# Softmax denominators inverted by pow on GpSimd instead of a reciprocal on VectorE, in a kernel whose engine orders come from a cost model

## Chip, cores, metric

One core of one Trainium2 chip. The metric is the device time of one execution in microseconds. Timed runs of the kernel before and of the other kernel alternate on the same chip. PE is TensorE, DVE is VectorE, ACT is ScalarE, POOL is GpSimd, SP is SyncE, whose sequencer ("the issue queue", SPq in the profile) issues every DMA of this kernel.

## The reference, cut to what matters

Two layers. Each is sliding-window attention (2048 tokens, 32 heads of 16, window 256) and a token-mixing MLP with 1792 hidden units; before each stands a layer norm (a double one for the MLP).

```python
scores = einsum("bhqd,bhkd->bhqk", q, k) * (Dh ** -0.5)
p = softmax(where(mask, scores, -1e9), axis=-1)          # the denominators are of this softmax
o = einsum("bhqk,bhkd->bhqd", p, v)
x = x + o @ wo
...
x = x + B(layernorm(x))                                  # w1, gelu, w2 over the token axis
```

## The kernel before

The program is a graph of some 2,400 operations. Each has a price (`cost`, and for a DMA `issue` and `lat`). A list scheduler simulates the engines with these prices and fixes the order of every engine; two tables of whole numbers (`RANK`, `MOVES`) then shift priorities and places. They look like the outcome of a search on the same prices, and I call them annealed; the search itself is not in the file. The program issues each engine's list in that order, with waits on semaphores. So a price is never executed: it only decides what stands behind what.

```python
def _pick(self, e, cand, ready, free, mode):   # which operation engine e takes next, by simulated time
...
o.end = free[e] = m + o.cost                   # the engine is held for the price
o.done = o.end + (o.lat if o.lat is not None else self.LAT[e])
...
def reorder(self, moves):
    for e, mv in zip(self.ENGS, moves):
        if mv:
            self.order[e] = [self.order[e][i + d] for i, d in enumerate(mv)]
...
for o in self.order[e]:                        # emit: in order, with waits
    for s, v in waits[o.idx]:
        eng.wait_ge(sem(s), v)
    ins = o.fn(eng)
```

The route of the denominators, once for each of 30 groups of heads and queries. P times V leaves numerators and denominators in PSUM; DVE copies both to SBUF (`cs`).

```python
o_rr = op("sync", ... rr[:, tr.slot, 0, :], cs[16:P:32, tc.slot] ..., dma=True, cost=300, lat=1400.0, issue=570.0)
for r in range(4):                             # second half of the heads up to its rows
    op("sync", ... cs[32*r+16:32*r+32, tc.slot, 0, :], cs[32*r:32*r+16, tc.slot, 1, :], dma=True, ..., after=[o_rr])
op("vector", lambda e: e.reciprocal(rr[:, tr.slot, 1, :], rr[:, tr.slot, 0, :]), cost=330)      # 128 x 32
op("sync", ... rscr <- rr[:, tr.slot, 1, :], dma=True)                                          # to DRAM
op("sync", ... md <- rscr broadcast to 16 rows each, dma=True)                                  # and back
op("gpsimd", lambda e: e.tensor_tensor(oT[:, to.slot, :], cs[:, tc.slot, 0, :], md[:, tm.slot, :], op=ALU.mult), cost=1400)
```

The tiles are few: 3 for `cs`, 2 each for `rr` and `md`, 7 for `oT`. GpSimd also makes the masked copies of the keys (`kbd`), `rstd` of every layer norm (with a pow of one or two elements) and some copies of V, all in one order with the output tiles `oT`.

The softmax here doesn't subtract the row's maximum and nothing guards it: scores larger than these inputs give would overflow.

Of the kernel before, what the change touches and what calls it, by code (L numbers as in the profile page):

```python
# [7 lines left out]
dt = mybir.dt  # L8
ALU = mybir.AluOpType
ACTF = mybir.ActivationFunctionType  # L10

P = 128
# [4 lines left out]
W2F, W2OUT = 2, (3, 7)  # L17
# [4 lines left out]
    38, 478, -248, -93, 7, 6, -38, -55, 0, -12, 14, -1, -14, 17, 7, 49, 0, 0, -11, -57, -29, 12, -32, 17, 163, -113,  # L22
    -26, 0, -76, 48, 174, -114, 0, -155, 72, 0, 0, 91, 0, -197, -108, 0, -146, 0, 0, -43, -29, -200, 193, 102, 0,
    116, -16, 0, -1, 11, -60, 21, -73, 18, 2, -2, 7, 89, 40, -31, -47, -15, 10, 0, -22, -49, 42, 322, -14, 6, 33, 2,
    0, 13, 12, 0, -17, -8, -15, 0, 5, -20, 0, 0, 0, -65, 142, 93, 62, -58, 23, 23, -51, -8, -30, 20, 27, 0, -36,
    -55, 10, 8, 0, 76, 151, 136, 83, -40, -3, -176, 115, -122, 460, -486, -53, -30, 29, 53, 0, -45, 0, 0, -39, -32,
    -78, 0, -2, 0, 0, 0, 0, 0, -52, 0, 0, 0, 0, 0, 0, 0, 19, -6, -13, -12, 0, -6, 4, -18, 0, 0, 7, 132, -19, -10,
    -13, 10, 103, -116, 115, -193, 419, 0, 41, 10, 1, 0, -10, 6, -14, -46, 5, -20, 0, 0, 103, -15, 11, 17, 0, 0, -6,
    -79, -112, -156, 0, -7, 0, -468, 0, 0, 0, 2, 0, 17, -7, 9, 6, 12, 0, -28, 0, 45, 117, 31, -17, 0, 0, 0, -19, -6,
    -107, -186, 167, -24, 82, 120, 248, 217, 122, 0, -3, 18, 55, -4, -27, 0, -6, 0, -120, 0, 1, 50, 52, 478, 268, 0,  # L30
    13, 47, 0, -11, 0, 113, 15, 46, 44, -30, -22, -52, 0, 14, -410, 20, 180, -153, -435, -439, 359, -7, 0, -3, 15,
    -10, 13, 10, -4, 12, 0, -86, -10, -52, -43, 17, 227, -51, -403, -135, -167, -266, -230, -240, 44, 0, 0, 4, -190,
    72, 0, 0, 0, 0, 3, 0, -1, 0, 0, 0, 0, 0, 0, 0, 0, 0, 0, 0, 0, 0, 0, 0, 0, 0, 0, 0, 0, 0, 6, 57,
# [3 lines left out]
        7, 1, 3, -2, -1, -1, 4, -1, -8, -1, 1, 3, 3, -4, 2, 3, 3, 0, 2, 2, -8, -8, 0, 0, 0, 0, 2, 0, -2, 0, 0, 2, 0,  # L37
        1, 1, 1, -5, 1, -1, 0, 0, 0, 0, 0, 0, 0, 0, 1, -1, 0, 0, 0, 0, 0, 0, 0, 0, 0, 0, 0, 0, 0, 0, 0, 0, 0, 0, 0,
        0, 0, 0, 0, 0, 0, 1, -1, 0, 0, 0, 0, 0, 0, 0, 0, 0, 0, 0, 0, 0, 0, 0, 0, 0, 0, 0, 0, 0, 0, 0, 0, 0, 0, 0, 0,
        0, 0, 0, 0, 0, 0, 0, 0, 0, 0, 0, 0, 0, 0, 0, 0, 0, 0, 0, 0, 0, 0, 0, 0, 0, 0, 0, 0, 0, 0, 0, 0, 0, 0, 0, 0,  # L40
        0, 0, 0, 0, 0, 0, 0, 0, 0, 0, 0, 0, 0, 0, 0, 0, 0, 0, 0, 0, 0, 0, 0, 0, 0, 0, 0, 0, 0, 0, 0, 0, 0, 0, 0, 0,
        0, 1, -1, 0, 0, 0, 0, 0, 0, 0, 0, 0, 0, 0, 0, 0, 0, 0, 0, 0, 0, 0, 0, 0, 0, 0, 0, 0, 0, 0, 0, 0, 0, 0, 0, 0,
        0, 0, 0, 0, 0, 0, 0, 0, 0, 0, 0, 0, 0, 0, 0, 0, 0, 0, 0, 0, 0, 0, 0, 0, 0, 0, 0, 0, 1, 1, -2, 0, 2, -1, -1,
        0, 1, 3, 3, 4, -4, 1, 4, 4, -5, 0, -8, 1, 1, 1, 2, 0, -8, 0, 2, 7, 7, 1, -4, -2, 4, -6, -3, 2, -4, -4, 0,
        27, -1, 10, 10, 4, 4, -5, -3, 6, -7, -7, 4, -7, 15, -4, 5, -5, -1, -12, 2, 2, 2, -5, -16, -6, -1, -7, 4, 1,
        -4, -4, -1, 0, 0, 0, 0, 0, 0, 0, 3, -1, 2, -1, 1, -4, 1, 1, -2, 0, 0, 1, -1, 0, 0, 0, 0, 0, 0, 0, 0, 0, 1,
        -1, 0, 0, 0, 0, 0, 0, 0, 0, 0, 0, 1, -1, 0, 0, 0, 0, 0, 0, 0, 1, -1, 0, 0, 1, -1, 0, 0, 0, 0, 0, 1, -1, 0,
        0, 1, 1, -2, 0, 0, 0, 0, 0, 0, 0, 0, 0, 0, 0, 0, 0, 0, 0, 0, 0, 0, 0, 1, -1, 0, 0, 0, 0, 0, 0, 0, 0, 0, 0,
        0, 0, 0, 0, 0, 0, 0, 0, 0, 0, 0, 0, 0, 0, 0, 0, 0, 0, 0, 0, 0, 0, 0, 0, 0, 0, 0, 0, 0, 0, 0, 0, 0, 0, 0, 0,
        0, 0, 0, 0, 0, 0, 0, 0, 0, 0, 0, 0, 0, 0, 0, 0, 0, 0, 0, 0, 0, 0, 0, 0, 0, 0, 0, 0, 0, 0, 0, 0, 0, 0, 0, 0,  # L50
        0, 0, 0, 0, 0, 0, 0, 0, 0, 0, 0, 0, 0, 0, 0, 1, -1, 0, 0, 0, 0, 0, 0, 0, 0, 0, 0, 0, 0, 0, 0, 0, 0, 0, 0, 0,
        0, 0, 0, 0, 0, 0, 0, 0, 0, 0, 0, 0, 0, 0, 0, 0, 0, 0, 0, 0, 0, 0, 0, 0, 0, 0, 0, 0, 0, 0, 0, 0, 0, 0, 0, 0,
        0, 1, -1, 0, 1, -1, 0, 1, -1, 0, 0, 0, 0, 0, 0, 0, 0, 0, 0, 0, 0, 0, 0, 0, 0, 0, 3, -1, -1, -1, 4, 0, -2,
        -1, 2, 0, -3, 0, 0, 1, -1, 1, -1, 3, -1, 2, -2, -2, 0, 2, -1, -1, 3, -1, 2, 2, -3, 6, 6, -5, -2, -2, -2, 2,
        2, -4, 1, 4, 0, 0, 2, -1, 1, 1, 1, 1, 1, -15, 1, -1, 3, 3, 3, 20, 3, 3, 0, -7, 1, -8, -8, 16, 7, -3, 1, 1,
        15, 0, 2, 5, -9, 11, -4, -11, -11, -11, -1, -6, 0, 0, 0, 2, -10, 2, -8, 4, 11, -3, 2, -3, 1, -4, -4, 0, 4,
        6, -2, 2, -6, 6, 6, -6, -2, -1, 9, -2, -10, -3, 1, 12, -3, -3, 2, -3, 8, 2, -5, -2, -6, -3, -2, -2, 1, -3,
        5, 0, -2, -1, -1, -1, 0, 0, 0,
    ),
    (  # L60
        7, 4, 4, -2, -4, 6, 6, 6, -4, 5, 6, 4, 7, 7, 3, -7, 2, 4, 4, 4, 4, 4, 5, 10, 24, 1, 3, 13, 3, 5, 0, 1, 4,
        -30, 5, 7, -8, -28, 8, 2, -2, -6, 1, 13, -7, -1, 1, 8, -3, 5, -1, -41, -2, -2, -2, 4, -54, 3, 8, 4, -2, 4,
        -1, -1, 3, 11, -9, 4, 1, -1, 4, -7, 1, 6, 1, 6, 4, 5, -25, -1, 3, 4, 5, 6, 0, 3, 4, 4, 4, -3, 3, 3, 4, -23,
        4, 4, 4, 0, -3, 2, 2, 2, 2, -26, -32, 1, 2, 2, 2, -2, -5, 1, -1, 2, -1, -1, 0, 1, 1, 1, -3, 0, 0, 0, 0, 0,
        1, -1, 0, 0, 0, 0, 0, 0, 0, 1, -1, 0, 0, 0, 1, 1, -2, 0, 1, 1, 1, 2, 0, -5, 1, -1, 0, 2, -1, -1, 0, 2, 0, 1,
        1, 2, -5, 1, 3, 0, 0, -5, 5, 1, -1, 1, 4, 2, -6, -1, 1, 2, 0, 2, 0, 1, 1, -12, 1, 2, -2, 2, 2, 2, -2, 1, 1,
        -7, 0, 0, 0, 0, 0, 0, 0, 1, -1, 0, 0, 0, 1, 1, 1, -3, 0, 0, 0, 2, 0, 1, -3, 0, 2, 0, 1, 3, -4, 3, 3, -2, 3,
        1, 3, 4, 0, 5, 3, 7, 3, 3, 5, 5, 5, -5, -15, -9, -20, -4, 2, 2, 4, 2, 0, -5, 1, 3, -7, -1, -1, 0, 1, 3, -2,
        -1, -1, 1, -1, 0, 0, 0, 0, 0, 0, 0, 1, -1, 0, 0, 0, 1, 1, -2, 0, 0, 0, 0, 1, -1, 0, 0, 0, 0, 0, 0, 0, 0, 0,
        1, -1, 0, 0, 0, 0, 0, 0, 1, 2, 2, 2, 3, 1, -4, -7, 0, 0, 0, 0, 1, -1, 1, -1, 0, 0, 0, 0, 0, 0, 0, 0, 0, 0,  # L70
        0, 0, 0, 0, 0, 0, 0, 0, 1, -1, 2, 0, 2, 3, 3, -5, -1, 5, 3, 1, 3, -8, 2, -5, 1, -6, 0, 0, 0, 0, 0, 2, 0, -2,
        0, 2, 0, 2, -3, -1, 0, 3, -1, -1, 1, 1, 2, 2, -1, -6, 0, 1, -1, 1, 1, -2, 0, 0, 2, 3, 1, 2, 2, 2, 3, 4, 6,
        6, -10, 8, 10, -5, -13, 1, 7, 7, -1, -7, 8, -11, -9, 7, 5, 7, -6, 6, -7, -4, 4, -13, -5, -2, -8, 0, 0, 1,
        -1, 0, 0, 0, 2, 0, -2, 0, 1, 1, 1, 5, 3, 1, 3, 4, 4, 1, 3, -7, 3, 1, -14, 1, 2, 4, -1, 3, -15, -2, 1, -3, 1,
        -1, 3, -1, 2, -2, 3, 3, -1, -1, -6, 1, 2, 2, -1, 2, 2, 4, -7, 0, 0, 1, 1, 1, -8, 0, 0, 0, 0, 2, -1, -1, 0,
        0, 1, 1, -2, 0, 1, -1, 0, 0, 0, 0, 2, 0, 1, 1, 1, 1, 1, 1, 3, 6, 4, 5, 0, 8, -14, 4, 2, 5, -5, 4, 6, -4, 2,
        5, 6, 6, 3, -17, 5, 5, 2, -22, 3, 6, -9, -8, -16, 4, 5, 7, -2, 6, 6, 7, 0, 7, -9, 6, 6, 0, -5, 0, 4, -17, 1,
        2, 2, -17, -16, 0, 0, 0, 0, 0, 1, -1, 0, 2, -1, -1, 0, 0, 0, 0, 0, 0, 0, 0, 0, 0, 1, 1, 1, 1, 1, 1, 1, 1, 2,
        2, 2, -2, 1, 2, 4, 1, 1, -3, 1, 3, 3, 0, 4, 1, -4, 2, -26, 1, -3, 3, 1, -2, 1, 1, 2, 0, -6, 0, 1, 1, 2, 2,
        2, -5, -3, 2, 0, -2, 2, 2, -2, 1, 1, -4, 0, 0, 2, 0, 1, -3, 3, 0, -2, -1, 0, 0, 0, 0, 0, 3, 1, -1, -3, 2, 0,  # L80
        3, 1, -1, 1, 1, 1, 1, 5, -10, -1, 1, 2, -3, -3, 2, 0, 2, 0, -4, 0, 6, 3, 3, 4, 4, 4, 4, -7, -6, -8, 1, -8,
        0, 0, 0, 0, 0, 9, 13, -1, 18, -2, 0, 0, -3, 2, 2, -10, 2, -9, 2, 3, -8, 2, -5, -10, 3, 4, 4, -6, -3, -1, -6,
        1, 1, -2, 2, -1, 2, 0, -3, 0, 0, 0, 0, 0, 0, 3, 0, 0, -3, 0, 0, 1, 1, 3, -3, 2, -1, -3, 1, -1, 0,
    ),
    (
        0, 0, 1, -1, 0, 0, 1, 1, -2, 1, -1, 0, 1, 3, 0, 0, -4, 0, 0, 0, 0, 0, 0, 0, 1, -1, 0, 0, 0, 0, 1, -1, 0, 0,
        0, 0, 0, 0, 0, 0, 0, 0, 1, -1, 0, 0, 0, 0, 0, 0, 0, 0, 0, 0, 0, 0, 0, 0, 0, 0, 0, 0, 1, -1, 0, 0, 0, 0, 0,
        0, 0, 0, 0, 0, 0, 0, 0, 0, 0, 0, 0, 0, 0, 0, 0, 0, 0, 0, 0, 0, 0, 0, 0, 0, 0, 0, 0, 0, 0, 0, 0, 0, 1, -1, 0,
        0, 0, 0, 0, 0, 0, 0, 0, 0, 0, 0, 0, 0, 0, 0, 0, 0, 0, 0, 0, 0, 1, -1, 0, 0, 0, 0, 0, 0, 1, -1, 0, 0, 0, 0,
# [449 lines left out]
def bass_interleave_layers__sliding_block__mixer_token_mlp__prompt_kernel(  # L539
# [21 lines left out]
    with es:  # L561
        sb = lambda name, shape, d=dt.bfloat16: es.enter_context(nc.sbuf_tensor(name, shape, d))
        NKU, NQU, NVU, NPT, NCS, NMD, NOT, NW1, NSTG = 9, 7, 5, 8, 3, 2, 7, 4, 3
        x_sb = sb("x_sb", [P, NT, D])
# [36 lines left out]
        g = Graph(nc, es)  # L601
# [512 lines left out]
```

## Time and profile before

| | before |
|---|---|
| median, range (7 runs of one session) | 484.32 us, 481.53 to 486.41 |
| PE, DVE, ACT, POOL busy in the profiled run (span 481.6 us) | 427.7, 370.0, 322.9, 137.2 us |
| PE idle (span less busy) | 53.9 us |
| granted PE clock | 0.993 |

The lines that carry the reading are in the prediction. One view more, the busy time by stretch, is needed to compare the attention stages (columns: stretch, length, then busy us and instructions for PE, weight load, DVE, ACT, POOL, then granted clock, DMA share, GB/s):

```profile
17.00:180.00 163.00, 134.57 (x2962) 67.41 (x2986) 144.40 (x296) 148.09 (x166) 57.57 (x73) 0.99 0.30 82
232.00:393.00 161.00, 146.52 (x2944) 73.87 (x2972) 136.65 (x281) 137.57 (x150) 52.95 (x69) 0.99 0.34 94
```

GpSimd works about a third of these stages.

### The profile page before, as it was taken

What the parts mean: (1) busy time and instruction counts of PE and PEld (TensorE: products, weight loads), DVE (VectorE), ACT (ScalarE), POOL (GpSimd) and SP (SyncE); (2) the same over time, 40 slices, a digit from 0 to 9 for tenths busy, and PEclk for the clock granted to TensorE, in tenths of its full rate; (3) what the DMA queues carried; (4) which work ended last, traced back from release to release, by engine and by line L of the source; (5) the groups of instructions that cost most, each with busy time, mean ns of one, the idle gap of its engine ahead of it and who ended that gap; (6) DMA issues with size and microseconds to landing.
All of it is one profiled execution on the core that took longest, in us unless ns stands there. A gap on an engine that the chain in (4) does not pass through costs nothing.

```text
span 481.6 us, 15631 instructions
## 1 busy us (share of the span) xinstructions
PE 427.7 (89%) x6763; PEld 209.6 (44%) x6831; DVE 370.0 (77%) x747; ACT 322.9 (67%) x367; POOL 137.2 (28%) x205
## 2 busy tenths in 40 slices
PE   7897887798889698999999899987989979999997
PEld 4453533353334344444554454434444434444443
DVE  6999988988988978665887888888997856951313
ACT  2899999998987860534878978996998862061000
POOL 4223435235422413024102443523374031200000
PEclk9999999999998999999999999998999999999999
DMA  8602221234243344331225422240335235424555
GB/s 243 184 3 71 65 84 39 65 102 134 77 117 109 84 119 121 88 88 44 78 60 129 112 78 71 75 114 9 101 108 167 81 107 163 126 71 120 175 153 176
DMA packets 83993, 49.47 MB, mean 103 GB/s; under 512 B 14676, under 2 KB 78164, under 8 KB 83924
## 3 DMA queue, kind: packets, MB, share of 16 engines
q1 hardware_dynamic: 83924, 48.46, 35.6%
q8 instruction: 54, 0.88, 0.8%
q14 instruction: 15, 0.12, 0.1%
HBM read 41.43 MB, written 2.59 MB: 91 GB/s over the span
## 4 chain that ended last, share of the span: by engine, by line
PE 60%; ACT 14%; DVE 11%; DMA 7%; SPq 3%; issue 3%; POOL 1%; POOLq 0%
PE PS L1037 18%; PE PS L1014 13%; ACT pt L863 13%; PE PS L767 6%; PE PS L896 6%; PE PS L968 5%; PE PS L851 5%; PE PS L797 4%; DVE cs L940 3%; DVE pt L879 2%; DMA cs<-cs 2%; DMA rr<-cs 2%; DVE pt L876 2%; SPq L946 1%; POOL oT L958 1%
## 5 line engine op out<-in xcount | busy, mean ns | idle before, releaser
L863 ACT ACTIVATE pt<-PS 128x1024 bf16<-128x1024 f32 (+1 forms) x304 | 283.9, 1032 | 39.5 <-PE PS L851 37.7
L1014 PE MATMUL PS<-xh_sb,w1b 128*128 128x512 bf16 x428 | 102.9, 380 | 9.3 <-DMA w1b<-in_B_w_dram 3.3
L1037 PE MATMUL PS<-ub,w2b 128*128 128x512 bf16 x429 | 100.6, 379 | 2.8 <-issue 1.3
L851 PE MATMUL PS<-qT,kbd 32*128 32x64 bf16 (+4 forms) x1632 | 61.0, 245 | 17.7 <-ACT pt L863 6.0
L958 POOL TENSOR_TENSOR oT<-cs,md 128x512 bf16<-128x512 f32 x30 | 40.4, 1347 | 100.7 <-DMA md<-rscr 46.3
L1014 PEld LDWEIGHTS PS<-xh_sb,w1b 128*128 128x128 bf16 x448 | 40.1, 98 | 58.8 <-issue 8.9
L1037 PEld LDWEIGHTS PS<-ub,w2b 128*128 128x128 bf16 x448 | 41.6, 98 | 51.1 <-issue 3.3
L879 DVE TENSOR_TENSOR pt<-pt,ldm 128x1024 bf16<-128x1024 bf16 (+1 forms) x80 | 58.4, 732 | 5.8 <-ACT pt L863 5.6
L767 PE MATMUL PS<-xhT,wqkv 128*128 128x512 bf16 x237 | 59.2, 380 | 3.4 <-issue 1.9
L783 POOL TENSOR_SCALAR kbd<-stg,par 128x512 bf16<-128x512 bf16 x56 | 46.0, 829 | 54.4 <-DVE stg L734 49.5
L1026 DVE TENSOR_TENSOR ub<-PS,ub 128x512 f32<-128x512 f32 x70 | 46.1, 684 | 16.5 <-PE PS L1014 16.3
L851 PEld LDWEIGHTS PS<-qT,kbd 32*128 32x128 bf16 x1632 | 23.4, 93 | 72.4 <-ACT pt L863 38.9
L1042 DVE SCALAR_TENSOR_TENSOR x_sb<-PS,bcol,x_sb 128x512 bf16<-128x512 f32 x32 | 23.1, 744 | 39.1 <-PE PS L1037 39.1
L1029 ACT ACTIVATE ub<-ub,bcol 128x512 bf16<-128x512 f32 x28 | 18.5, 713 | 47.2 <-DVE ub L1026 47.1
L940 DVE COPY cs<-PS 128x512 f32<-128x512 f32 x60 | 38.9, 682 | 10.6 <-PE PS L896 10.2
L896 PE MATMUL PS<-pt,vt 64*18 64x64 bf16 (+4 forms) x3040 | 40.9, 248 | 5.7 <-DVE qT L734 1.7
L694 POOL TENSOR_SCALAR rstd<-agg 128x2 f32<-128x2 f32 (+1 forms) x40 | 9.8, 246 | 120.8 <-DVE agg L691 119.8
L689 DVE BATCH_NORM_STATS2 stats<-x_sb 128x6 f32<-128x512 bf16 x64 | 42.7, 681 | 1.1 <-DMA x_sb<-in_A_x_dram 0.6
L876 DVE TENSOR_TENSOR pt<-pt,ldm 128x512 bf16<-128x512 bf16 (+1 forms) x104 | 41.1, 412 | 2.1 <-ACT pt L863 1.7
L896 PEld LDWEIGHTS PS<-pt,vt 64*18 64x18 bf16 x3040 | 32.1, 86 | 16.9 <-DVE pt L876 4.1
L968 PE MATMUL PS<-wo_sb,oT 128*128 128x512 bf16 x118 | 30.9, 388 | 4.8 <-POOL oT L958 2.8
L767 PEld LDWEIGHTS PS<-xhT,wqkv 128*128 128x128 bf16 x256 | 21.8, 98 | 29.5 <-issue 3.3
(54 smaller groups left out, 328.1 us busy)
## 6 DMA issues: line engine op xcount, KB each, us to landing
w1b<-in_B_w_dram SPq DMA_DIRECT2D x56, 256.0 KB, 3.1
w2b<-in_B_w_dram SPq DMA_DIRECT2D x112, 128.0 KB, 2.4
md<-rscr SPq DMA_DIRECT2D x30, 256.0 KB
cs<-cs SPq DMA_DIRECT2D x120, 32.0 KB, 2.8
out_dram<-x_sb SPq DMA_DIRECT2D x16, 128.0 KB, 1.8
x_sb<-in_A_x_dram SPq DMA_DIRECT2D x3, 512.0 KB
wqkv<-in_A_wqkv_dram SPq DMA_DIRECT2D x2, 384.0 KB, 6.5
x_sb<-in_A_x_dram SPq DMA_DIRECT2D x4, 128.0 KB, 2.2
```

The costliest lines, as they stand in the source:

```text
L767: mm_group(ft, 4, lambda e, c: e.matmul(PS[:, ft.slot, :], lhsT=wqkv[:, c, which * 512 + o * P:which * 512 + (o + 1) * P], rhs=xhT[:, tx.s ...
L783: op("gpsimd", lambda e, h=h: e.tensor_scalar(kbd[:, tk[o].slot, :, h, :], stg[:, ts.slot, :].rearrange("p (s n) -> p s n", n=64), par[:, ...
L851: last = e.matmul(PS[:, bank(r), c0 * 64:(c0 + nb) * 64], lhsT=kbd[32 * r:32 * r + 32, tkk.slot, jj, :, :].rearrange("p h n -> p (h n)"), ...
L863: return e.activation(pt[:, tp.slot, 2 * u:2 * u + 2, 0:n], PS[:, b0:b0 + 2, 0:n], ACTF.Exp, scale=SMSCALE)
L876: return e.tensor_tensor(v, v, msk.unsqueeze(1).to_broadcast([P, 4, w]), op=ALU.mult)
L879: return e.tensor_tensor(v, v, msk.unsqueeze(1).unsqueeze(1).to_broadcast([P, 4, k, w]), op=ALU.mult)
L896: last = e.matmul(PS[32 * r:32 * r + 18, tO[h].slot, q0 * 64:(q0 + nb) * 64], lhsT=vt[64 * h:64 * h + 64, tvv.slot, jj, 4 * o + r, :], rhs ...
L940: op("vector", lambda e, tO=tO[h], tc=tc, h=h: e.tensor_copy(cs[:, tc.slot, h], PS[:, tO.slot, :]), reads=[tO[h]], writes=[(tc, h)], cost= ...
L968: mm_group(ft, 4, lambda e, o, i=i, ft=ft: e.matmul(PS[:, ft.slot, :], lhsT=oT[:, tos[o][0].slot, i * P:(i + 1) * P], rhs=wo_sb[:, o, :], ...
L1014: out_ = e.matmul(PS[:, tu.slot, :], lhsT=w1b[:, tw.slot, s, tt * P:(tt + 1) * P], rhs=xh_sb[:, 4 * m + s, :], start=(n == 0 and s == 0), ...
L1026: op("vector", lambda e, tu=tu, ft=ft: e.tensor_tensor(uacc(ft), PS[:, tu.slot, :], uacc(ft), op=ALU.add), reads=[tu] + uk(ft), writes=uk( ...
L1037: mm_group(ft, NFT, lambda e, fc: e.matmul(PS[:, ft.slot, :], lhsT=w2b[:, tws[fc // W2F].slot, fc % W2F, k * P:(k + 1) * P], rhs=uT(fc), s ...
```

## The change

The intent: DVE is near 87% busy in the attention and stands in front of reciprocals; GpSimd has time. So the reciprocal becomes a pow with exponent -1 on GpSimd, priced at 1800 ns. At the same time the prices of the DMA issues are refitted, and the order tables are annealed anew for these prices. Cut to its core (the tables, some 2,750 integers, are left out):

```diff
-    WINDOW = ({0: 400.0, 1: 300.0, 2: 50.0}, {0: 100.0, 1: 250.0, 2: 100.0})
+    WINDOW = ({0: 400.0, 1: 400.0, 2: 0.0}, {0: 100.0, 1: 250.0, 2: 50.0})
+        mone = sb("mone", [P, 1], dt.float32)
+        op("gpsimd", lambda e: e.memset(mone[:], -1.0), writes=["mone"])
-                   writes=[(tr, 0)], dma=True, cost=300, lat=1400.0, issue=570.0, prio=len(g.ops))
+                   writes=[(tr, 0)], dma=True, cost=200, lat=1400.0, issue=610.0, prio=len(g.ops))
-                       ... dma=True, cost=120, lat=1600.0, issue=380.0, ...      # copies of the second half
+                       ... dma=True, cost=120, lat=1850.0, issue=575.0, ...
-                op("vector", lambda e, tr=tr: e.reciprocal(rr[:, tr.slot, 1, :], rr[:, tr.slot, 0, :]), reads=[(tr, 0)],
-                   writes=[(tr, 1)], cost=330, prio=-1e5)
+                op("gpsimd", lambda e, tr=tr: e.tensor_tensor(rr[:, tr.slot, 1, :], rr[:, tr.slot, 0, :],
+                                                              mone[:].to_broadcast([P, 32]), op=ALU.pow),
+                   reads=[(tr, 0), "mone"], writes=[(tr, 1)], cost=1800)
-               dma=True, cost=1000, lat=2000.0, issue=390.0, ...                 # w1 loads
+               dma=True, cost=1000, lat=1900.0, issue=450.0, ...
-                    cost=340 * W2F, lat=1700.0, issue=390.0, ...                 # w2 loads
+                    cost=340 * W2F, lat=1400.0, issue=480.0, ...
```

## The prediction

> **What bounds the kernel now.** The program runs on one core, so I read four things in this order: the busy shares, the chain that ended last, the list of waits, and the timeline around the longest waits. First the page and its chain:
>
> ```profile
> PE 427.7 (89%) x6763; PEld 209.6 (44%) x6831; DVE 370.0 (77%) x747; ACT 322.9 (67%) x367; POOL 137.2 (28%) x205
> ...
> PE 60%; ACT 14%; DVE 11%; DMA 7%; SPq 3%; issue 3%; POOL 1%; POOLq 0%
> ...
> L949 DVE RECIPROCAL rr<-rr 128x32 f32<-128x32 f32 x30 | 10.3, 344 | 8.3 <-DMA rr<-cs 8.3
> ```
>
> PE is busy for 427.7 of 481.6 us, so at most 481.6 - 427.7 = 53.9 us can be won without less matmul work. The table of busy time by stretch says where those are: in the attention of the first layer (17 to 180 us) PE works 134.6 of 163 us and idles 28.4; in that of the second (232 to 393 us) 146.5 of 161, idling 14.5; from 393 to 412 us it idles 3.1; the MLP stretches (180 to 232, 412 to the end) lose 1.6 and 3.7. In the two attention stages DVE is busy 144.4 and 136.7 us and ACT 148.1 and 137.6, so three engines are near 85 to 91% together and none alone is the bound: each stall in order on DVE shows up on PE a little later. That is where the change works.
>
> The reciprocal is a small row (30 x 344 ns = 10.3 us), but DVE also stands still for it for 8.3 us, as it takes its instructions in order and the row waits for a DMA. The chain shows what that does, in the stretch 319 to 330 us (columns: start, length, what):
>
> ```profile
> 321.85 0.27 DVE x_sb L1042
> 322.12 3.95 DMA rr<-cs
> 326.07 0.02 issue
> 326.09 0.35 DVE rr L949
> 326.44 0.58 DVE x_sb L1042
> 327.02 0.05 issue
> 327.07 0.40 PE PS L750 x4
> ```
>
> The DMA that gathers the denominators was issued at 322.12, DVE stood before the reciprocal until 326.09, the next layer's row block on DVE came after it, and PE waited for that. The timeline gives the cost to PE here and in two like places:
>
> ```profile
> 327.07 0.40 PE L750 MATMUL PS<-ident,xh_sb 128*128 128x128 bf16 x4 [2.05 <-DVE x_sb L1042]
> ...
> 143.00 1.04 PE L1014 MATMUL PS<-xh_sb,w1b 128*128 128x512 bf16 x3 [1.70 <-DVE ub L1026]
> ...
> 395.00 0.35 DVE L949 RECIPROCAL rr<-rr 128x32 f32<-128x32 f32 x1 [4.11 <-DMA rr<-cs]
> ...
> 394.92 1.89 PE L1014 MATMUL PS<-xh_sb,w1b 128*128 128x512 bf16 x8 [2.67 <-DMA w1b<-in_B_w_dram]
> ```
>
> The bracket is the idle time before the instruction and what ended it. So PE lost 2.05 and 1.70 us behind reciprocals that were ordered too early, and 2.67 us for a weight tile whose load stood in the single DMA issue queue behind the denominators' transfers.
>
> **What the Trainium skill says.** "VectorE: DVE Perf Modes", section "First, the fixed hardware budget", says reciprocal is a hardware iterative divide on DVE. It gives no price for that; the trace's 344 ns for 32 elements is one. "GPSIMD Engine Reference", section 3.1, describes GpSimd's elementwise kernels as software loops with a fixed dispatch and then a cost per element. The trace agrees for pow, which this kernel already uses for rstd: undisturbed rows take 0.55 us with one element and 0.69 with two, so 0.14 us for one element more. "SBUF — State Buffer", section "Who interferes with whom", says that a DVE instruction with two SBUF inputs and a GpSimd one that reads SBUF exclude each other, the later one blocking fully. The trace agrees for long GpSimd instructions:
>
> ```profile
> 140.79 1.27 POOL L958 TENSOR_TENSOR oT<-cs,md 128x512 bf16<-128x512 f32 x1 [11.90 <-DMA cs<-cs]
> ...
> 141.11 1.23 DVE L876 TENSOR_TENSOR pt<-pt,ldm 128x512 bf16<-128x512 bf16 x1
> ```
>
> The mask takes 0.41 us alone and 1.23 here: it ended 0.28 us after the GpSimd instruction. But a mask (L879) that began 0.24 us into a two-element pow took its usual 0.69 us, so pow's short reads did not hold it. Whether 32 elements do, no row of this kernel shows.
>
> **The change part by part.**
> 1. Thirty reciprocals leave DVE. Removed: 30 x 344 ns = 10.3 us busy and the 8.3 us of standing before them. Of the latter, PE felt 2.05 + 1.70 = 3.75 us. Of the busy time I count DVE's ratio of chain to busy, 0.11 x 481.6 / 370.0 = 14%, so 1.5 us.
> 2. Thirty pows arrive on GpSimd. The model prices them at 1.8 us; the slope of the trace's two sizes gives 0.41 + 32 x 0.14 = 4.9 us. The model's price would come from a loop that overlaps its elements, the other from one that does not; I cannot tell which holds, and lean to the author having priced it (60 to 40). GpSimd goes from 137.2 to about 191 us (40% of the span), or to 284 (59%). It is not a bound in sum either way. On the path they lie only at the ends of the attention stages, where the last output tile from this route releases the projection (in the second layer the copy-back landed and GpSimd ran at 404.19, PE at 405.52). Each end grows by 1.8 - 0.34 = 1.5 us, or by 4.6. The first end now waits for another transfer (cs to cs), so part is hidden: I take 2 us for both.
> 3. The lock. DVE starts 80 + 104 masks and 64 normalisations, 248 in the 324 us of the two stages, 0.77 per us. If a 1.8 us pow held the port throughout, the first of them would stand on average 1.8 - (1 - exp(-0.77 x 1.8)) / 0.77 = 0.8 us, times 30 = 25 us of DVE. With the 14% of above 3.5 us on the path; as the two-element pow held nothing I take half, 1.8.
> 4. Issue times in the model. It had 380 ns for the copies of the upper half, and the trace has 568 (120 times); for the weight loads 390. The new values, 575 and 450 to 480, are what such traces show, so the fixed orders should collide less: the 2.67 us at 394.9 is of this kind, and from the other 53.9 - 3.75 - 2.67 = 47 us of PE idle I choose 3 us, for a new annealing on truer prices.
> No matmul, exponential or transfer is added or dropped; the priority and order tables only move them.
>
> Sum: -3.75 - 1.5 - 2.67 - 3 + 2 + 1.8 = -7.1 us. From the median 485.88 that is 478.8; I say 479.
>
> **The rivals.**
> - The pow is slow (4.9 us) and holds the port. Then the same formula gives 3.6 us a time, 109 us of DVE, which has only 163 + 161 - 144.4 - 136.7 = 43 us free in the attention: DVE becomes the bound and the time goes to 495 or more. For it: the slope of 0.14 us. Against it: two-element pows hold nothing, and orders annealed for a much wrong price would hardly be kept.
> - The denominators' route is hidden anyway: the three places are chance and the new orders have others like them; ACT, which waits 37.7 us for scores, takes over. Then 483 to 486. For it: no engine alone is the bound, so a gain on one is diluted.
> - The annealing, with true prices, removes much more of the 43 us PE idles in attention. A quarter of it gives about 472.
>
> **Range and chances.** The three runs of before lie 1.1% apart, which alone makes 3 us either way. Taking the middle course as likeliest, the rival with more at a fifth, the slow pow with a held port under a tenth: 471 to 488 us. Two per cent faster is 476.2; I give that 0.22. Within two per cent 0.70, slower 0.08.
>
> **What would show it.** Right: no reciprocal row on DVE, DVE busy near 360 us, no DVE wait for rr, pow rows near 1.8 us, PE busy unchanged near 428 and its idle time down by some 7 us, most of it in the attention stages. Wrong: pow rows of 4 to 5 us, masks on DVE whose mean rises from 412 and 732 ns as they stand behind pow, or output tiles on GpSimd later than before at the ends of both attention stages with PE waiting for them; or PE idle time as before in other places, which would mean that only the place of the waits moved.

## The result, and the profile after

The changed kernel took 532.12 us (median of 4, 530.12 to 533.71), the kernel before 483.91 us (480.46 to 487.47) beside it. The ratio is 1.099, interval 1.090 to 1.109: 10% slower, far outside my range. A ratio here is the mean time of one kernel's fast runs over that of the other's of the same rounds, so not quite the ratio of the medians quoted.

The page after (busy; the chain by engine; the new row; two old rows to compare):

```profile
PE 441.8 (83%) x6767; PEld 212.7 (40%) x6835; DVE 361.5 (68%) x718; ACT 324.7 (61%) x366; POOL 295.3 (56%) x236
...
PE 39%; POOL 26%; DVE 10%; DMA 9%; issue 7%; ACT 5%; SPq 4%; POOLq 0%; ACTq 0%
...
L950 POOL TENSOR_TENSOR rr<-rr,mone 128x32 f32<-128x32 f32 x30 | 164.2, 5475 | 39.6 <-DMA rr<-cs 37.1
...
L880 DVE TENSOR_TENSOR pt<-pt,ldm 128x1024 bf16<-128x1024 bf16 (+1 forms) x80 | 53.5, 682 | 4.4 <-ACT pt L864 4.4
...
L877 DVE TENSOR_TENSOR pt<-pt,ldm 128x512 bf16<-128x512 bf16 (+1 forms) x104 | 40.0, 402 | 2.8 <-ACT pt L864 2.4
```

One pow takes 5.48 us in the mean (5.41 in the median), three times its price. GpSimd goes from 137.2 to 295.3 us busy, and from 1% of the chain that ended last to 26%. The masks on DVE did not get longer: 682 and 402 ns, against 732 and 412 before.

The waits after (engine and line, what it waited for: us in total, times, longest us), and the same ones before:

```profile
ACT pt L864 <- PE PS L852: 81.8, 74, 8.5
POOL rr L950 <- DMA rr<-cs: 37.1, 14, 5.3
DVE xh_sb L701 <- POOL rstd L697: 28.0, 12, 9.4
PE PS L751 <- DVE xh_sb L701: 8.1, 2, 6.0
PE PS L852 <- POOL kbd L784: 5.6, 2, 4.4
SPq L953 <- POOL rr L950: 94.1, 22, 9.0
```

```profile
ACT pt L863 <- PE PS L851: 37.7, 51, 4.5
DVE xh_sb L700 <- POOL rstd L696: 2.9, 5, 1.3
SPq L951 <- DVE rr L949: 17.5, 11, 3.8
```

The waits of DVE for `rstd` rose from 2.9 to 28.0 us, the stands of the issue queue for the inverted denominators from 17.5 to 94.1 us, and ACT waits 44 us more for scores. All of them are engines that take their list in order, behind something that comes later than the list expects.

A stretch of the timeline shows one case from end to end:

```profile
85.84 5.58 POOL L950 TENSOR_TENSOR rr<-rr,mone 128x32 f32<-128x32 f32 x1 [0.79 <-DMA rr<-cs]
...
87.27 0.16 DVE L692 BATCH_NORM_AGGREGATE agg<-stats 128x2 f32<-128x6 f32 x1
...
91.52 0.19 POOL L695 TENSOR_SCALAR rstd<-agg 128x2 f32<-128x2 f32 x1
...
91.79 0.69 POOL L697 TENSOR_TENSOR rstd<-rstd,mhalf 128x2 f32<-128x2 f32 x1
...
92.52 1.11 DVE L701 TENSOR_SCALAR xh_sb<-x_sb,agg,rstd 128x512 bf16<-128x512 bf16 x2 [5.08 <-POOL rstd L697]
...
94.15 1.27 DVE L941 COPY cs<-PS 128x512 f32<-128x512 f32 x2
...
95.48 0.61 PE L852 MATMUL PS<-qT,kbd 32*128 32x256 bf16 x8 [3.47 <-DVE cs L941]
```

The last of the statistics (`agg`) was there at 87.4 us, but `rstd` stood behind a pow until 91.52. DVE, in order, stood for 5.08 us before the normalisation. The copies that free PSUM stood behind it on DVE, and PE lost 3.47 us before its next scores.

The attention stages after, as the table before:

```profile
17.00:199.00 182.00, 137.06 (x2947) 67.20 (x2972) 136.74 (x272) 148.80 (x165) 137.86 (x90) 0.94 0.28 76
245.00:443.00 198.00, 164.46 (x3036) 80.42 (x3064) 142.17 (x285) 145.25 (x156) 131.25 (x93) 0.96 0.29 79
```

The two stages went from 163 and 161 us to 182 and 198, and hold more than the whole loss. No engine is full in them, GpSimd neither (137.9 of 182, 131.3 of 198). In sum: PE idle rose from 53.9 to 532.0 - 441.8 = 90.2 us, and PE busy by 14.1 us at a granted clock of 0.955 (before 0.993); the traces miss about the same number of matmul records (6767 and 6763).

And the port, which my prediction feared. A mask that begins inside a pow:

```profile
97.48 5.49 POOL L950 TENSOR_TENSOR rr<-rr,mone 128x32 f32<-128x32 f32 x1 [1.46 <-DMA rr<-cs]
97.62 0.46 DVE L877 TENSOR_TENSOR pt<-pt,ldm 128x512 bf16<-128x512 bf16 x1
```

It took 0.46 us, where 0.41 is usual, and ended 5 us before the pow did. Counting in the trace, 52 masks of L877, 27 of L880 and 9 normalisations of L701 began inside a pow. Shape by shape, the means inside a pow and with GpSimd idle are 416 and 415 ns (L877, 128x512), 682 and 681 (L880, 128x1024), 403 and 403 (L701). Those of the same three lines that began inside the multiplication of an output tile (L960; 5, 6 and 3 of them, shapes mixed) have means of 835, 959 and 1145 ns, so the count would show a hold. Shown by the trace alone: the pow held none of these 88 DVE instructions.

### The profile page after: what moved, and what is told of

The parts are those of the page before. It is cut to its first block, busy times and chain, and to the rows that moved or that the text cites. A ratio compares the mean times of both kernels' runs of the same rounds, so it can differ in the third digit from the quotient of the medians.

```text
span 532.0 us, 15641 instructions
## 1 busy us (share of the span) xinstructions
PE 441.8 (83%) x6767; PEld 212.7 (40%) x6835; DVE 361.5 (68%) x718; ACT 324.7 (61%) x366; POOL 295.3 (56%) x236
## 4 chain that ended last, share of the span: by engine, by line
PE 39%; POOL 26%; DVE 10%; DMA 9%; issue 7%; ACT 5%; SPq 4%; POOLq 0%; ACTq 0%
POOL rr L950 17%; PE PS L1016 13%; PE PS L1039 13%; DMA cs<-cs 4%; ACT pt L864 3%; POOL kbd L784 3%; PE PS L970 3%; PE PS L768 3%; POOL oT L960 3%; DVE cs L941 2%; PE PS L897 2%; PE PS L798 2%; DMA rr<-cs 2%; PE PS L852 2%; SPq L947 2%
## 5 line engine op out<-in xcount | busy, mean ns | idle before, releaser
L950 POOL TENSOR_TENSOR rr<-rr,mone 128x32 f32<-128x32 f32 x30 | 164.2, 5475 | 39.6 <-DMA rr<-cs 37.1
L1016 PE MATMUL PS<-xh_sb,w1b 128*128 128x512 bf16 x425 | 111.0, 401 | 22.9 <-ACT md L926 5.0
L1039 PE MATMUL PS<-ub,w2b 128*128 128x512 bf16 x430 | 101.9, 382 | 3.3 <-DVE pt L877 1.5
L1016 PEld LDWEIGHTS PS<-xh_sb,w1b 128*128 128x128 bf16 x448 | 41.8, 102 | 78.4 <-issue 17.4
L768 PE MATMUL PS<-xhT,wqkv 128*128 128x512 bf16 x237 | 62.3, 395 | 10.1 <-DVE xh_sb L701 4.0
L784 POOL TENSOR_SCALAR kbd<-stg,par 128x512 bf16<-128x512 bf16 x56 | 43.9, 791 | 31.7 <-DVE stg L735 31.5
L960 POOL TENSOR_TENSOR oT<-cs,md 128x512 bf16<-128x512 f32 x30 | 39.1, 1305 | 34.2 <-DMA md<-rscr 18.4
L880 DVE TENSOR_TENSOR pt<-pt,ldm 128x1024 bf16<-128x1024 bf16 (+1 forms) x80 | 53.5, 682 | 4.4 <-ACT pt L864 4.4
L701 DVE TENSOR_SCALAR xh_sb<-x_sb,agg,rstd 128x512 bf16<-128x512 bf16 x64 | 28.0, 458 | 28.1 <-POOL rstd L697 28.0
L877 DVE TENSOR_TENSOR pt<-pt,ldm 128x512 bf16<-128x512 bf16 (+1 forms) x104 | 40.0, 402 | 2.8 <-ACT pt L864 2.4
```

Of the source, the lines that this page charges most:

```text
L768: mm_group(ft, 4, lambda e, c: e.matmul(PS[:, ft.slot, :], lhsT=wqkv[:, c, which * 512 + o * P:which * 512 + (o + 1) * P], rhs=xhT[:, tx.s ...
L784: op("gpsimd", lambda e, h=h: e.tensor_scalar(kbd[:, tk[o].slot, :, h, :], stg[:, ts.slot, :].rearrange("p (s n) -> p s n", n=64), par[:, ...
L880: return e.tensor_tensor(v, v, msk.unsqueeze(1).unsqueeze(1).to_broadcast([P, 4, k, w]), op=ALU.mult)
L950: op("gpsimd", lambda e, tr=tr: e.tensor_tensor(rr[:, tr.slot, 1, :], rr[:, tr.slot, 0, :], mone[:].to_broadcast([P, 32]), op=ALU.pow), re ...
L960: op("gpsimd", lambda e, tm=tm, to=to, tc=tc: e.tensor_tensor(oT[:, to.slot, :], cs[:, tc.slot, 0, :], md[:, tm.slot, :], op=ALU.mult), re ...
L1016: out_ = e.matmul(PS[:, tu.slot, :], lhsT=w1b[:, tw.slot, s, tt * P:(tt + 1) * P], rhs=xh_sb[:, 4 * m + s, :], start=(n == 0 and s == 0), ...
```

## The experiments

Theory S: the loss is the pow's length. Theory O: the new orders are bad whatever it takes. Theory L: the port (the trace spoke against it). Seventeen runs. (A division on GpSimd, which would have kept the result right with another instruction, was not accepted when the kernel was built; no run records it.) Where an operation is moved to another engine, that is done in the finished order lists, so every other operation keeps its place. All results here are medians of timed runs, of the fast ones where some were slow (a run over 1.5% above the fastest of its kernel counts as slow). Profiles are from fast runs, but for the length of the pow in a_pow20.

**a_mult: a short instruction in the pow's place.**

```diff
-  op("gpsimd", ... rr[:, tr.slot, 0, :], mone[:].to_broadcast([P, 32]), op=ALU.pow), ... cost=1800)
+  op("gpsimd", ... rr[:, tr.slot, 0, :], mone[:].to_broadcast([P, 32]), op=ALU.mult), ... cost=1800)
```

> The changed kernel with the pow of each denominator tile replaced by a multiplication by -1 on the same engine, in the same place, with the same operands and waits. The result is wrong on purpose. Theory S (the slow pow, 5.41 us each, is the loss; it delays what follows it in order on GpSimd and the denominators' route): the row falls below 0.4 us and the time falls by most of the 48 us, to 472 to 490 us. Theory O (the new orders of all engines are bad by themselves, whatever the pow takes): the time stays above 510 us. Theory L (the pow holds the port that VectorE shares and blocks its masks): also falls to about 485, but then the masks must have been longer in the changed kernel, which its rows do not show (682 and 402 ns, before 732 and 412).

476.9 us, ratio 0.985 (0.981 to 0.989). The row took 0.24 us. Theory O falls: with these orders the program can be 1.5% faster than before; all 55 us between 476.9 and 532.1 are the pow's length. So it is not the place on GpSimd that costs, it is the time there. (The result is wrong, so this is a bound and no kernel.)

**a_dve: the new orders, reciprocals on DVE.**

```diff
+  for (o, tr), k in zip(recs, (93, 102, 119, ...)):     # where the denominators landed in the trace
+      g.order["gpsimd"].remove(o)
+      o.eng, o.fn = "vector", lambda e, tr=tr: e.reciprocal(rr[:, tr.slot, 1, :], rr[:, tr.slot, 0, :])
+      at.setdefault(k, []).append(o)                     # inserted into g.order["vector"] at k
```

> The changed kernel with its new orders, but each reciprocal back on VectorE, put into the VectorE order where the denominators landed in the trace. Theory S: GpSimd has 164 us less to do, time 475 to 490 us, within 2% of the kernel before. Theory O: above 510 us. Whether the new orders with refitted issue times are worth the 3 us that I gave them shows in whether it lies under the kernel before.

484.5 us, ratio 1.003 (0.996 to 1.010), correct. Theory S again. With the reciprocals back on DVE the new orders show no gain; against a_mult they lose 7.6 us. The places of the reciprocals were mine, taken from the trace with the slow pows; others were not tried.

**a_occ: GpSimd held, route short.**

```diff
 (as a_dve, and at each old pow's place)
+  extra_op("gpsimd", lambda e, n=n: e.tensor_tensor(junk[:, n % 4, :], two[:], mone[:].to_broadcast([P, 32]), op=ALU.pow),
+           <the transfer that brings the denominators>, k)
```

> As a_dve, but at the place of each old pow GpSimd runs a pow of 32 constants that nobody reads, released by the same transfer. So GpSimd is held as long as in the changed kernel while the denominators' route is as short as in a_dve. If the loss is that other GpSimd work (keys, rstd, output tiles) stands behind the pow: 515 to 532 us. If the loss is the length of the route (5.4 us longer from denominators to output tile, and the issue queue standing for it): 480 to 495 us.

514.6 us, ratio 1.062 (1.057 to 1.067): 30 of the 48 us. Just under the range that I gave for GpSimd being held: by itself this gives most of the loss, but not all. Its wait row for `rstd` is near that of the change (28.0):

```profile
DVE xh_sb L703 <- POOL rstd L699: 23.0, 12, 8.2
```

**a_lat: route long, GpSimd free.**

```diff
 (as a_dve, and for each transfer of the reciprocals to the scratch)
+  x.deps.append(g.order["scalar"][k])     # also wait for the ScalarE instruction that ended ~5.4 us after the reciprocal
```

> As a_dve (484.5 us; reciprocals on VectorE), but each transfer of the reciprocals to the scratch also waits for a ScalarE instruction that ended about 5.4 us after the reciprocal in the trace of a_dve. GpSimd runs nothing more; only the route is longer, by about what the pow adds (5.07 us), and the issue queue stands with it. With a_occ at 514.6 us, 30.1 over a_dve, the changed kernel's other 17.5 us should be this: 495 to 508 us. If the two causes overlap (each alone already gives most): 510 us or more. If the route's length costs nothing: 484 to 489 us.

537.7 us, ratio 1.110 (1.103 to 1.116). My subtraction (17.5 us left for the route) was wrong: the longer route alone loses as much as the change. The delay came out somewhat larger than planned, as ACT itself falls behind and the wait with it: from the reciprocal to the issue of its transfer 6.8 us in the mean over the 30, in the changed kernel 5.7 from the pow's start. So its 53 us over a_dve are too high for the route's part by an amount that I did not measure. With the 30 us of a_occ they make far more than the 48 us of the change: either the two ways overlap, or a_lat overstates its own. In either case the orders bear neither well.

**b_pow: the old orders, only the engine swapped.**

```diff
+  g.order["vector"].remove(o)
+  o.eng, o.fn = "gpsimd", <pow>           # inserted where the reciprocal began in the trace
```

> The kernel before with its own orders and prices; only each reciprocal is moved to a pow on GpSimd, placed in the GpSimd order where the reciprocal began in the trace. Theory S: the loss is there without new orders, 520 us or more (more than the change, as nothing was ordered around it). Theory O: within 2% of the kernel before, 475 to 493 us.

589.3 us, ratio 1.215 (1.209 to 1.221), granted clock 0.896. Even dearer than the change. The new orders had a place planned for a pow, here I put it in by hand; b_pow9 has the same difference.

**a_pow9: the pow as long as its price.**

```diff
-  rr[:, tr.slot, 1, :], rr[:, tr.slot, 0, :], mone[:].to_broadcast([P, 32]), op=ALU.pow
+  rr[:, tr.slot, 1, 0:9], rr[:, tr.slot, 0, 0:9], mone[:].to_broadcast([P, 9]), op=ALU.pow
```

> The changed kernel with its pow over the first 9 of the 32 elements only (the rest stays at a constant set once; the result is wrong on purpose). From 5.41 us for 32 and 0.69 for 2, the slope is 0.152 us per element and 9 elements should take 1.75 us, nearly the 1.8 us for which the new orders were made. Theory S with the mis-sized price as the failed step: 478 to 486 us, that is near the 479 predicted for that price and within a few us of the 476.9 with the multiplication. If the loss were proportional to the pow's length: 0.30 of the way from 476.9 to 532, so 492 us.

478.6 us, ratio 0.992 (0.985 to 0.998), wrong result. The row (median 1.79 us):

```profile
L950 POOL TENSOR_TENSOR rr<-rr,mone 128x9 f32<-128x9 f32 x30 | 56.6, 1887 | 58.6 <-DMA rr<-cs 58.6
```

That this is the 479 us predicted is in part luck: I had counted 7.1 us, or 1.5%, from a median of 485.9, and the gain here is 0.9% (0.2 to 1.5). The cost is not proportional to the length: by the ratios, the first 1.55 us of pow over a_mult cost 0.6%, some 3 us, and the next 3.6 us another 10.8%, some 52 us.

**a_pow20: between.**

```diff
+  (as a_pow9, with 0:20)
```

> The changed kernel with its pow over the first 20 elements only (wrong result on purpose). By 5.41 us for 32 and 1.79 for 9, 20 elements take 3.52 us. Time with 0.24 us is 476.9, with 1.79 us 478.6, with 5.41 us 532. If slack in the orders takes up what is near the price and each us beyond is paid in full: a straight line from the price, 478.6 + 53.4 x (3.52 - 1.79) / (5.41 - 1.79) = 504 us. If there is more slack than that: under 495 us.

490.8 us in its three fast runs (492.9 with a slow one), ratio 1.015 (1.008 to 1.022; wrong result), with 3.5 us per pow (read in the slow run). The loss is convex, that is, each further microsecond costs more than the one before: from 1.8 to 3.5 us it costs 12 us, from 3.5 to 5.4 another 41. The straight line of my expectation (504) was wrong too; the orders have more slack at first and none later.

**b_pow9: old orders, pow of 1.8 us.**

```diff
+  (as b_pow, with 0:9)
```

> The kernel before with its own orders and its reciprocals as pows on GpSimd of 9 elements (1.79 us; wrong result on purpose), to be set against a_pow9, which has the new orders. If the new orders are what makes room for a pow of the price assumed: 490 us or more. If a pow of 1.79 us fits anywhere: 478 to 484 us.

507.7 us, ratio 1.048 (1.042 to 1.054; wrong result). With the same pow the new orders take 478.6, 29 us less. They were made for a 1.8 us pow, and worked for it; here it stands where the reciprocal did. The 29 us are those of the whole planning: order tables, refitted DMA prices and the pow's place.

**n_dve, n_18, n_54, n_18_9: the price alone.** The changed kernel's program without the annealed tables, so that only the price decides the orders.

```diff
-  RANK = ( 38, 478, ... )
+  RANK = ()
-  g.reorder(MOVES)
 (n_dve: reciprocal on "vector", cost=330; n_18: pow, cost=1800; n_54: pow, cost=5414; n_18_9: n_18 with a pow of 9 elements)
```

> The changed kernel's program without its annealed tables (no ranks, no moves), with the reciprocal on VectorE: the plain list scheduling. The base of the next two. Without the tables I expect 490 to 520 us.

> As n_dve, but the pow on GpSimd, priced at the change's 1800 ns. Whatever the theory, slower than n_dve by a good part of the 48 us: 25 to 80 us over it.

> As n_18, but the pow priced at its measured 5414 ns, so that the scheduler orders every engine around it. If the loss is that the orders were made for a wrong price: within 8 us of n_dve. If a 5.41 us step in this route costs whatever the order: still 15 us or more over n_dve, and near n_18.

> As n_18 (plain list scheduling, pow priced at 1800 ns), but the pow takes 9 elements and so 1.79 us, what it is priced at (wrong result on purpose). If the loss of n_18 comes from the gap between price and length: 484 to 498 us, near n_dve's 491.1 and under n_54's 501.8. If those orders are bad whatever the pow: above 520 us.

491.1 us (ratio 1.012), 569.6 (1.173), 501.8 (1.033) and 492.7 (1.017; wrong result). This answers what a_occ and a_lat left open: whether a busy GpSimd and a long route must cost this much. n_18 and n_54 run the same work, and differ in one number of the model. With the true price 67.8 of the 78.5 us over n_dve are gone, though GpSimd is as busy as in the changed kernel (profile of n_54) and the route as long (from the pow's start to the issue of its transfer 5.7 us in the mean, in n_18 5.5). DVE waits 16.0 us for `rstd` in n_54 and 41.4 in n_18.

```profile
PE 428.4 (86%) x6769; PEld 208.6 (42%) x6831; DVE 371.5 (75%) x717; ACT 324.7 (65%) x367; POOL 295.1 (59%) x236
```

What is left, 501.8 - 491.1 = 10.7 us, lies between my two expectations (within 8, or 15 and more): the true price does not buy it off in this plain scheduling. Each price gave one order, and how far plain orders scatter by chance was not measured. New tables annealed for 5.41 us were not tried, so whether they would take the rest back is open. The model also keeps each GpSimd operation, for its price, apart from the normalisations on DVE (`ported`), which the pow did not hold in the trace; whether some of the 10.7 us is this was not tested. n_18's orders are good when the pow is as long as they believe (n_18_9). So most of the loss is the gap between price and length (six sessions, in which the kernel before took 483.3 to 484.9 us):

| orders made for | pow in the run | time, us |
|---|---|---|
| annealed, 1.8 us | 0.24 us (mult) | 476.9 |
| annealed, 1.8 us | 1.8 us | 478.6 |
| annealed, 1.8 us | 3.5 us | 490.8 |
| annealed, 1.8 us (the change) | 5.4 us | 532.1 |
| plain, 1.8 us | 1.8 us | 492.7 |
| plain, 1.8 us | 5.4 us | 569.6 |
| plain, 5.4 us | 5.4 us | 501.8 |
| plain, reciprocal on DVE | 0.34 us | 491.1 |

**a_spmove: transfers moved in the issue queue.** In the changed order, the transfer to the scratch and the one back were put 2 to 6 places later in the issue queue; further was impossible, as the order became a cycle of waits.

```diff
+  (tag "late" on both transfers; each re-inserted into g.order["sync"] 2 to 6 places later)
```

> The changed kernel with one edit of the issue queue's order: the transfer of the reciprocals to the scratch and the one back stand 2 to 6 places later, so that weight loads and copies go out in the pow's shadow (94 us of standing for the pow in the changed kernel's queue). All else as in the changed kernel. If the route's length costs through the transfers behind it in the queue: 500 to 520 us. If it costs through the output tiles coming late, or through GpSimd: 525 to 540 us.

595.9 us, ratio 1.229 (1.223 to 1.234). It went the other way. The stand was only exchanged for another one: the loads now ahead stood for weight buffers that PE had not freed (93.4 us, in the changed kernel 50.1), and the route waited behind them.

```profile
SPq L985 <- PE PS L1016: 93.4, 25, 15.9
```

So it says nothing for or against the queue as the carrier of a_lat's loss. Which share of the route's cost goes through the issue queue and which through late output tiles stays open.

**a_newton: a correct, shorter inverse on GpSimd.**

```diff
-  <pow>
+  r = magic - bits(d)                      # int32 subtraction, first guess
+  b = d * r; b = 2 - b; r = r * b          # twice; seven instructions, each waits for the one before
```

> The changed kernel with each pow replaced by seven short GpSimd instructions (an integer subtraction for a first guess and two Newton steps), in the pow's place, with a wait between each two. The result should be correct. The multiplication of this size took 0.24 us, so I expect 7 times 0.24 plus 6 waits of about 0.1, some 2.3 us in all. Theory S: 478 to 488 us and so a correct form of the change that costs no more than the kernel before; under 2% from it either way. Theory that GpSimd must not be in the route at all: above 500 us.

482.4 us, ratio 0.998 (0.993 to 1.002), correct. One inverse takes 2.3 us in the median from its first instruction to the end of its last. So GpSimd may well be in the route, if the work is short. It repairs the change and gains nothing over the kernel before.

**b_norec, b_late, b_late3: what the reciprocals on DVE were worth.** b_norec takes the reciprocals out of the kernel before; the two others move some of them later on DVE.

```diff
 b_norec
-  rscr[te.slot] ... <- rr[:, tr.slot, 1, :]
+  rscr[te.slot] ... <- rr[:, tr.slot, 0, :]       # and the 30 reciprocals removed from the order
 b_late (b_late3 without the last pair)
+  for n, k in {11: 2, 23: 4, 26: 2, 29: 7}.items():   # reciprocal n goes k places later on "vector"
```

> The kernel before without its reciprocals: the transfer to the scratch reads the plain denominators (wrong result on purpose), nothing runs in the reciprocal's place. It bounds what step 1 of the prediction (10.3 us of VectorE and the stands before them) could give with the old orders. By my working 5.3 us plus part of the 2.67 us wait for the weight tile: 476 to 480 us, ratio 0.983 to 0.992. If the stands are hidden anyway (rival): ratio 0.995 or more.

> The kernel before with four of its thirty reciprocals, those before which VectorE stood (1.30, 2.06, 0.82 and 4.11 us), moved 2 to 7 places later in the VectorE order; nothing else. If the stands cost PE what the timeline showed (1.70, 2.05 and part of 2.67 us): 478 to 482 us, ratio about 0.99. If the places are chance and the loss only moves: ratio 0.997 to 1.003.

> As b_late, but the reciprocal at 395.0 us in the end of the second attention stays where it was; only the three others are moved later. In b_late that one went behind work that waited for a weight tile whose load stood behind it in the issue queue, and PE waited 8.0 us for such tiles against 3.3 before. If that was b_late's loss of 1.6%: ratio 0.990 to 1.000. If moving the others costs too: above 1.005.

b_norec: 480.2 us, ratio 0.993 (0.989 to 0.997; wrong result). b_late: 489.6, ratio 1.016 (1.009 to 1.022). b_late3: 484.9 in its four fast runs, ratio 1.000 (0.994 to 1.006). The stands that I had read as PE's loss give nothing back when the reciprocals are moved behind other work. The one at the end of the attention was even in the right place: moved, it stood behind work that waited for weights whose load stood behind it in the issue queue (b_late, then before):

```profile
PE PS L1015 <- DMA w1b<-in_B_w_dram: 8.0, 3, 3.5
```

```profile
PE PS L1014 <- DMA w1b<-in_B_w_dram: 3.3, 2, 2.7
```

No correct version beat the kernel before by more than its interval.

## Why the prediction was wrong, point by point

- **Step 2 failed, the price of the pow.** I had two numbers, 1.8 us from the diff and 4.9 from the slope of the profile, and leaned 60 to 40 to the diff because its author would have priced it. The runs show 5.41 us, and 1.79 for 9 elements. The slope of the profile was right and a little low: 0.69 us for 2 elements and 5.41 for 32 make 0.157 us per element. A clue in the kernel before was overlooked: it prices its small pows at 500 ns and 40 ns per element, so 540 and 580, where the trace has 0.55 and 0.69 us. The same formula gives 1,780 ns for 32 elements, close to 1800; whether the price came from there is not on record.
- **Also in step 2: where a longer pow would cost.** I let it cost only at the ends of the attention stages (4.6 us each). It costs wherever an order holds `rstd`, keys, output tiles or transfers behind it: a_occ alone gives 30 us, and the longer route of a_lat more than the whole loss. With 5.41 us and no lock my own sum would have been -3.75 - 1.5 - 2.67 - 3 + 2 x 5.07 = -0.8 us, so 485 us and not 532: the price was wrong, and so was the path by which it costs. A fixed share of the chain cannot give it either, as the cost is convex (some 3, then 12, then 41 us).
- **The rival was half right.** It had a slow pow and 495 us or more, which happened, but it had them through the port, which did not: Step 3's term of 1.8 us is zero, as 88 DVE instructions of the three lines counted began inside pows and none was held. My argument against this rival, that orders annealed for a wrong price would hardly be kept, was an argument about people and not from the profile.
- **Step 1 was not borne out.** 5.25 us predicted for DVE; b_norec, with the old orders, gave 0.7% or 3.4 us (by its interval 1.3 to 5.5, so too large by the middle value, but not clear of the noise). At 143.00 us I charged 1.70 us of PE to a reciprocal before which DVE stood 1.30 us; the mask after it took 1.23 us and not 0.41, as it met a multiplication on GpSimd, so part of the wait has that cause. And b_late3 shows that the stands of 1.70 and 2.05 us before PE were not to be had by moving the reciprocals out of the way.
- **Step 4 is neither shown nor refuted.** All steps together were to give 1.5%; a_pow9, where the pow is as long as the orders believe, gave 0.9% (0.2 to 1.5), and its 478.6 us against my 478.8 owe their closeness to a high base. That the split of the sum is right is not shown: in a_dve the new orders gain nothing with reciprocals on DVE.
- **Two slips of reading.** PE works 83% of the first attention stage, not 85% or more; and of the 248 DVE starts of step 3, 226 lie in the two stages. Neither moves the sum by a microsecond.

## What to carry to other kernels

When orders are made from prices, a price that is too low for an operation which others stand behind can cost far more than that engine's share of the chain suggests: here 3.6 us too little on each of 30 pows cost some 52 us, most of it for the last 1.9 us. Before an operation is moved to another engine, take its duration there from a trace, or from the slope between two sizes already in the trace, and trust that over the number in the model. And a wait seen in front of an instruction is a gain only if what comes after it has nothing else to wait for; move the instruction and see.

## What the Trainium skill lacked or had wrong

- "GPSIMD Engine Reference", section 3.1, prices the add of two tensors and has no number for pow. Here a pow of float32 took 0.55 us for 1, 0.69 for 2, 1.79 for 9, 3.5 for 20 and 5.41 us for 32 elements per partition, 0.157 us per element from 2 to 32, while a multiplication of 32 took 0.24 us.
- "SBUF — State Buffer", sections "Who interferes with whom" and "Summary: rules for kernel authors", has a GpSimd instruction that reads SBUF and a DVE one with two SBUF inputs exclude each other, the second waiting until the first has finished. That held for the 1.27 us multiplication (a mask of 0.41 us took 1.23), but not for pow, which reads SBUF too: 79 masks began inside pows of 5.4 us and took their usual time (at most 0.46 us for 128x512 and 0.73 for 128x1024).
- "VectorE: DVE Perf Modes" says how the reciprocal works and not what it costs: 344 ns for 32 float32 elements per partition.
- "Perfetto Trace Analysis", section "GPSIMD Engine Instruction", calls GpSimd spans unreliable. For the pow they agree with the spacing of starts: in the changed kernel the next GpSimd instruction began within 0.1 us of the pow's end 24 times, in the median 5.40 us after the pow's start, and the median span is 5.41 us.
